# Some small steps of the softmax and of exp(q) from VectorE to ScalarE, with another order of work, in an attention plus gated MLP kernel

## The chip, the core and the metric

The kernel runs on one core of one Trainium2 chip. The metric is device time in microseconds (us) of one execution, as the median of several runs. The core's engines run side by side, each through its own queue in order: TensorE (PE in the profile; PEld is its weight load), VectorE (DVE), ScalarE (ACT), GpSimd (POOL) and SyncE (SP), which issues nearly all DMAs here. An engine that waits for another one stalls everything behind the waiting instruction in its own queue.

## The reference

Attention over 4 batches, 8 heads, 576 tokens and head size 64, with a causal softmax and a compressive memory, and then an MLP with a piecewise activation over the 2304 tokens (512 to 2048 to 512).

```python
scores = q @ k.T / 8, causal mask; scores -= scores.max(-1)
a = exp(scores); a /= a.sum(-1) + 1e-9; local = a @ v
q_p = where(q > 0, q, exp(q) - 1) + 1
mem_out = (q_p @ M_prev) / (q_p . z_prev + 1e-6)
x = g * mem_out + (1 - g) * local          # g = sigmoid(beta), per head
h = x @ w_in
g2 = where(h >= 1, h, where(h <= -1, 0, (h + 1)**2 / 4))
out = g2 @ w_out
```

## The kernel before

Every product is done in pairs of float16 halves: a float32 operand is scaled by a power of two, rounded to a high half, and the remainder is the low half; three matmuls (high by high, high by low, low by high) replace one. The scaling and the splitting are elementwise work for ScalarE (`mul`, line 107, with the engine "act": a Copy with a scale) and VectorE (`sub_scaled`, line 114).

The work is cut into jobs. There are 8 **pairs** (two units each) and 16 **units** (two heads of one batch each). `prep` (line 311) prepares a pair: squares for the scales, halves of k, q, v and the memory, and phi(q) with its normalisation, whose first steps stand at lines 347 to 352: Exp of q on ScalarE, the minimum with 1 on VectorE (line 350), then max(q + 1, that) on VectorE. Four times a unit, `front` (line 430) makes one tile of scores: matmuls and a mask on PE, a maximum over the row on VectorE (lines 444 and 462), `negmax` (line 421, its instruction is line 424) that multiplies the negated maxima, two, four or one number per partition, by the pair's scale, and `expsum` (line 426), the exponential on ScalarE with those maxima as its bias. `back` (line 487) makes the high and low halves of the probabilities by `halves` (line 480): the high half on ScalarE, except for row groups 6 and 7 (the 128x512 pieces of the fourth tile), whose high half is on VectorE by the table `OPT`, and then the low half on VectorE. A DMA transposes the halves, and `pv1` and `pv2` multiply them by the values. `half_a` of a unit does tokens 0 to 255, `half_b` the other 320.

The weights come in 8 groups (`weight_group`, line 178): three integer steps on VectorE for each of two matrices turn the input's 64-bit words into float32 (lines 201 to 203), ScalarE sums squares, and then come the halves. The MLP runs in 9 **chunks** of 256 tokens; `chunk_prep` makes a chunk's halves, and for each weight group `mlp_h` (line 634) does 24 matmuls into the tile h (line 646) and evicts it by a Relu and a Square on ScalarE (lines 651 and 652), a step on VectorE that also reads h (line 653), and the two halves of g; `mlp_o` (line 658) does 12 matmuls with g. The tile h has one buffer only: the next 24 matmuls wait until both readers of h are done.

The string `PROGRAM` (line 38) names the jobs in the order in which the program writes them: l load, P prep, A and B the halves of a unit, W a weight group, p chunk preparation, c a chunk (c0/4 is its first four weight groups alone). This isn't the order in which they run: `in_order` (line 906) takes all instructions, prices each with a table of costs, and lists them anew for every engine by 24 passes of a list schedule, forward and backward, and keeps the best of them. What the written order fixes is the first ranking, and the turns in which jobs take the buffers of a ring (`Rings`, line 83).

Of the kernel before, what the change touches and what calls it, by code (L numbers as in the profile page):

```python
# [20 lines left out]
AF = mybir.ActivationFunctionType  # L21
ALU = mybir.AluOpType
# [9 lines left out]

BLENDS = (-0.1,) * 24

OPT = dict(whi="act", phi="act", ghi="act", hi={6: "dve", 7: "dve"})


PROGRAM = ("l0 l1 P0 W0 A0 A1 P1 A2 A3 p0 W1 B0 W2 B1 W3 c0/4 B2 B3 p1 W4 l2 c1/4 W5 W6 W7 c0 c1 P2 A4 A5 l3 P3 "
           "A6 A7 l4 p2 B7 B4 B5 P4 c2 l5 B6 A9 p3 P5 c3 A8 l6 A10 A11 p4 B8 B9 P6 c4 B10 B11 l7 p5 P7 c5 A12 "
           "A14 A15 A13 B13 p6 B14 c6 B15 B12 p7 c7 p8 c8")  # L40

P = 128
D = 64
# [6 lines left out]
def infini_moe_kernel(ctx: ExitStack, tc, qt, kt, qz, vm, beta, w, out):  # L50
# [6 lines left out]
    nc = tc.nc  # L57
    NPP, _, _, S = qt.shape
# [44 lines left out]
    def kind(job, c):  # L103

        notes.append((len(nc.cur_bb.bb.instructions), job, c))

    def mul(n, o, i, s):
        if n == "act":
            return nc.scalar.activation(o, i, AF.Copy, scale=s)  # L109
        if n == "pool":  # L110
            return nc.gpsimd.tensor_scalar(o, i, s, 1.0, op0=ALU.mult, op1=ALU.mult)
        return nc.vector.tensor_scalar(o, i, s, None, op0=ALU.mult)

    def sub_scaled(o, i, s, hi):

        nc.vector.scalar_tensor_tensor(o, i, s, hi, op0=ALU.mult, op1=ALU.subtract)  # L116
# [61 lines left out]
    def weight_group(r):  # L178
# [36 lines left out]
        for m, wt in enumerate(words):  # L215
            reg, s = group(m, r), wsc[:, m, r:r + 1]
            hi, lo = reg[:, :, 0, :], reg[:, :, 1, :]
            wt = wt.rearrange("p (c f) -> p c f", f=reg.shape[3])
            mul(OPT["whi"], hi, wt, s)
            sub_scaled(lo, wt, s, hi)  # L220
# [90 lines left out]
    def prep(u):  # L311
        p, job = u.p, u.job
# [33 lines left out]

        kind(job, "ph")
        fe = sb.tile([P, 2, 9, D], F32, name=f"fe{p}", tag="pn")
        nc.scalar.activation(fe, u.qr, AF.Exp)
        nc.vector.tensor_scalar(fe, fe, 1.0, None, op0=ALU.min)  # L350
        ft = u.qr
        nc.vector.scalar_tensor_tensor(ft, u.qr, 1.0, fe, op0=ALU.add, op1=ALU.max)
        kind(job, "pz")
# [29 lines left out]
        fs = ft.rearrange("p u s d -> p (u s) d")  # L383
        mul(OPT["phi"], pn[:, :, 0, :], fs, 1.0)
        nc.vector.tensor_tensor(pn[:, :, 1, :], fs, pn[:, :, 0, :], op=ALU.subtract)
# [30 lines left out]
    def stats(u):  # L416
        if "st" not in u.e:
            u.e["st"] = sb.tile([P, 3, 9], F32, name=f"st{u.n}", tag="st")
        return u.e["st"]

    def negmax(u, a, m):

        st = stats(u)
        nc.vector.tensor_scalar(st[:, 0, a:a + m], st[:, 0, a:a + m], u.pair.cs, None, op0=ALU.mult)  # L424

    def expsum(u, e, s, z):
        st = stats(u)
# [52 lines left out]
    def halves(u, hi, lo, e, z):  # L480
        r = stats(u)[:, 2, z:z + 1]
        kind(u.job, "ah")
        mul(OPT["hi"].get(z, "act"), hi, e, r)
        kind(u.job, "al")
        sub_scaled(lo, e, r, hi)

    def back(u, i):
# [27 lines left out]
        else:  # L515
# [4 lines left out]
            kind(u.job, "ah")  # L520
            mul(OPT["hi"].get(8, "act"), flat[:, 0:S], e, r)
            kind(u.job, "al")
# [111 lines left out]
    def mlp_h(c, r, a, tb):  # L634
# [18 lines left out]
        nc.vector.scalar_tensor_tensor(tm, h, tb[:, 0, j:j + 1], tm, op0=ALU.max, op1=ALU.min)  # L653
        mul(OPT["ghi"], g16[:, 0], tm, tb[:, 3, j:j + 1])
        sub_scaled(g16[:, 1], tm, tb[:, 3, j:j + 1], g16[:, 0])
# [43 lines left out]
    preps, gens = {}, {}  # L699
    for n, t in enumerate(PROGRAM.split()):  # L700
        f, arg = t[0], t[1:]
# [20 lines left out]
        else:  # L722
            c, _, cuts = arg.partition("/")
# [100 lines left out]
def shape(ins):  # L824

    rd, wr = operands(ins)
    return 1 if rd[0].ap[0][1] == D else 2 if wr[0].ap[0][1] == D else 0


def graph(prog):  # L830

    before, banks = None, set()
    cost, needs, written, read = [], [], collections.defaultdict(list), collections.defaultdict(list)
    for k, ins in enumerate(prog):
        rd, wr = operands(ins)
        c, b = estimate(ins, rd, wr, before)
        if ins.engine.name == "PE":
            before = b
        cost.append(c)
        need = set()  # L840

        banks |= {a.tensor.name for a in rd + wr if a.space == bass.MemoryType.PSUM}
        spans = [(span(a), False) for a in rd if a.space != bass.MemoryType.DRAM] + \
                [(span(a), True) for a in wr if a.space != bass.MemoryType.DRAM]
        for (name, p0, p1, bits), w in spans:
            for j, a0, a1, m in written[name]:
                if a0 < p1 and p0 < a1 and m & bits:
                    need.add(j)
            if w or name in banks:
                for j, a0, a1, m in read[name]:  # L850
                    if a0 < p1 and p0 < a1 and m & bits:
                        need.add(j)
        for (name, p0, p1, bits), w in spans:
            if w:
                for acc in (written, read):
                    acc[name] = [x for x in acc[name] if x[1] < p0 or x[2] > p1 or x[3] & ~bits]
                written[name].append((k, p0, p1, bits))
        for (name, p0, p1, bits), w in spans:
            if not w:
                read[name].append((k, p0, p1, bits))  # L860
        need.discard(k)
        needs.append(need)
    return cost, needs
# [42 lines left out]
def in_order(tc, notes):  # L906

    prog, tags = [], []
    notes = iter(notes + [(math.inf, "", "")])
    tag, after = ("", ""), next(notes)
    for k, i in enumerate(tc.nc.cur_bb.bb.instructions):
        while k >= after[0]:
            tag, after = after[1:], next(notes)
        if (i.ins or i.outs) and type(i).__name__ not in ("InstRegisterMove", "BassTilePoolBoundary"):
            prog.append(i)  # L920
            tags.append(tag)
    n = len(prog)
    cost, needs = graph(prog)
    users = [[] for _ in prog]
    for k, need in enumerate(needs):
        for j in need:
            users[j].append(k)
    engine = [i.engine.name for i in prog]
    turns = ["Transpose" in type(i).__name__ for i in prog]
    mode = [shape(i) if e == "PE" else 0 for i, e in zip(prog, engine)]  # L930

    def forward(urgency):
        lane = busy = 0.0
        window, warm = 0, False

        def hold(e, k, at):
            nonlocal lane, busy, window, warm
            if e == "SP":
                at += 75 if needs[k] else 25
                lane = max(at + cost[k][0] + 650, lane) + cost[k][1]  # L940
                if turns[k]:
                    return lane, max(at + cost[k][0] + 525, lane - 952)
                return lane, max(at + cost[k][0], lane - AHEAD)
            took = cost[k]
            if e == "PE":
                while at >= (window + 1) * WINDOW:
                    warm = busy > 0.85 * WINDOW or warm and busy > 0.4 * WINDOW
                    busy = 0.0
                    window += 1
                if not warm:  # L950
                    took = 2 * took - 3 if took > 25 else 55
                busy += took
            return at + took, at + took

        return listed(n, engine, mode, [len(x) for x in needs], users, urgency, hold, lambda a, b: HOP[a][b], 650.0)

    def backward(urgency):
        def hold(e, k, at):
            if e == "SP":
                end = at + cost[k][1]  # L960
                return end + cost[k][0] + 725, max(end, at + 75 + cost[k][0] * 0.3)
            return at + cost[k], at + cost[k]

        return listed(n, engine, mode, [len(x) for x in users], needs, urgency, hold, lambda a, b: HOP[b][a], 0.0)

    urgency = [k - PRIO.get(c, 0) - PRIO.get(job, 0) - PRIO.get(job + c, 0) for k, (job, c) in enumerate(tags)]
    best, order = math.inf, None
    for blend in BLENDS:
        times, taken = forward(urgency)
        end = max(t[1] for t in times)  # L970
        if end < best:
            best, order = end, taken
        back, _ = backward([-t[1] for t in times])
        middle = sum(t[0] for t in times) / n
        urgency = [blend * (t[0] - middle) - b[1] for b, t in zip(back, times)]
    last = {}
    for k in order:
        e = engine[k]
        if e in last:
            tc.add_manual_dep(prog[k], last[e], mybir.DependencyInfo(mybir.DependencyClass.NoSync, mybir.DependencyReason.DATA), reason="order")  # L980
        last[e] = prog[k].name
# [46 lines left out]
```

## Time and profile before

| | us |
|---|---|
| median of 3 runs | 617.37 (616.97 to 619.64) |
| the profiled execution | 617.87 |
| its span, first to last instruction | 616.2 |

The profile's numbers are of the profiled execution, in us from the start of its span. A busy time is a recorded one; records of neighbours on DVE and ACT overlap a little, so what an instruction takes from its engine's time is the distance from its start to the start of the next one, where nothing waits. The granted clock is the share of full speed (2.4 GHz) that TensorE had; 0.5 is its lower level of 1.2 GHz.

### The profile page before, as it was taken

What the parts mean: (1) busy time and instruction counts of PE and PEld (TensorE: products, weight loads), DVE (VectorE), ACT (ScalarE), POOL (GpSimd) and SP (SyncE); (2) the same over time, 40 slices, a digit from 0 to 9 for tenths busy, and PEclk for the clock granted to TensorE, in tenths of its full rate; (3) what the DMA queues carried; (4) which work ended last, traced back from release to release, by engine and by line L of the source; (5) the groups of instructions that cost most, each with busy time, mean ns of one, the idle gap of its engine ahead of it and who ended that gap; (6) DMA issues with size and microseconds to landing.
All of it is one profiled execution on the core that took longest, in us unless ns stands there. A gap on an engine that the chain in (4) does not pass through costs nothing. (4 is left out here: it accounts for less than half of the span.)

```text
span 616.2 us, 11580 instructions
## 1 busy us (share of the span) xinstructions
PE 521.7 (85%) x4481; PEld 333.6 (54%) x4481; DVE 475.5 (77%) x1106; ACT 451.8 (73%) x916; POOL 2.5 (0%) x12
## 2 busy tenths in 40 slices
PE   0324565768699999999999999999999999999996
PEld 0112334444456566656665665666666666666663
DVE  5999999999999998497989849978677763223221
ACT  5768877769989987599797879769886765444433
POOL 1000000000000000000000000000000000000000
PEclk9997655799899999999999999999999999999999
DMA  7885984795542945348473526904362531000000
GB/s 307 294 273 135 231 207 126 201 216 212 145 103 62 183 95 97 91 124 199 134 160 63 112 59 154 220 3 83 69 106 50 126 67 32 35 1 2 35 0 35
DMA packets 130792, 74.68 MB, mean 121 GB/s; under 512 B 122289, under 2 KB 122289, under 8 KB 128689
## 3 DMA queue, kind: packets, MB, share of 16 engines
q1 hardware_dynamic: 130736, 73.94, 48.3%
q8 instruction: 35, 0.57, 0.4%
q14 instruction: 21, 0.16, 0.1%
HBM read 38.80 MB, written 4.72 MB: 71 GB/s over the span
## 5 line engine op out<-in xcount | busy, mean ns | idle before, releaser
L646 PE MATMUL h<-xh,w 128*128 128x256 f16 x1728 | 207.5, 276 | 12.8 <-DVE tm L653 12.1
L663 PE MATMUL o<-w,g 128*128 128x512 f16 x864 | 207.8, 379 | 6.7 <-DVE g L116 3.8
L646 PEld LDWEIGHTS <-w 128*128 128x128 f16 x1728 | 170.1, 99 | 51.3 <-issue 20.1
L663 PEld LDWEIGHTS <-g 128*128 128x128 f16 x864 | 80.7, 98 | 88.0 <-DVE g L116 5.3
L653 DVE SCALAR_TENSOR_TENSOR tm<-h,tb,tm 128x512 f32<-128x512 f32 x72 | 53.8, 747 | 68.7 <-ACT tm L652 64.2
L651 ACT ACTIVATE tm<-h,tb 128x512 f32<-128x512 f32 x72 | 55.8, 775 | 68.3 <-PE h L646 68.1
L428 ACT ACTIVATE e<-s,st,sc 128x256 f32<-128x256 f32 (+4 forms) x144 | 91.4, 638 | 13.4 <-DVE st L424 9.1
L116 DVE SCALAR_TENSOR_TENSOR an<-e,st,an 128x512 f16<-128x512 f32 (+4 forms) x160 | 80.8, 538 | 6.9 <-ACT an L109 6.9
L109 ACT ACTIVATE g<-tm,tb 128x512 f16<-128x512 f32 x72 | 51.8, 721 | 26.6 <-DVE tm L653 24.6
L116 DVE SCALAR_TENSOR_TENSOR g<-tm,tb,g 128x512 f16<-128x512 f32 x72 | 53.5, 746 | 18.9 <-ACT g L109 18.7
L109 ACT ACTIVATE an<-e,st 128x128 f16<-128x128 f32 (+3 forms) x112 | 56.0, 544 | 11.5 <-DVE st L478 3.8
L413 PE MATMUL s<-ks,qs 64*128 64x256 f16 (+3 forms) x384 | 43.4, 335 | 23.9 <-ACT e L428 8.8
L462 DVE TENSOR_REDUCE st<-s 128x2 f32<-128x256 f32 (+1 forms) x64 | 52.0, 816 | 5.5 <-PE s L458 5.3
L533 PEld LDWEIGHTS <-vs 128*64 128x64 f16 x1024 | 40.6, 118 | 17.0 <-issue 16.6
L652 ACT ACTIVATE tm<-tm 128x512 f32<-128x512 f32 x72 | 45.3, 629 | 1.0
L413 PEld LDWEIGHTS <-qs 64*128 64x128 f16 x384 | 16.1, 101 | 48.2 <-issue 27.3
L428 ACT ACTIVATION_READ_ACCUMULATOR e<-s,st,sc 128x1 f32 x144 | 28.9, 201 | 0.0
L533 PE MATMUL v<-eb,vs 128*64 128x256 f16 (+1 forms) x384 | 24.2, 276 | 2.1 <-DMA eb<-an 2.1
L533 PE MATMUL v<-pt,m 128*64 128x256 f16 (+1 forms) x192 | 19.2, 271 | 7.0 <-DMA pt<-pn 4.0
L307 PE MATMUL s<-sc,ones 128*128 128x4 f32 (+1 forms) x32 | 6.0, 263 | 21.9 <-ACT m L328 13.7
L109 ACT ACTIVATE w<-w,wsc 128x1024 f16<-128x1024 f32 x15 | 17.2, 1144 | 7.9 <-DVE nr L362 5.6
L204 ACT ACTIVATE stg<-w 128x1024 bf16<-128x1024 f32 x15 | 15.8, 1051 | 6.6 <-DVE w L203 6.4
(154 smaller groups left out, 575.7 us busy)
## 6 DMA issues: line engine op xcount, KB each, us to landing
stg<-w SPq DMA_DIRECT2D x16, 1024.0 KB, 5.5
rn<-qz SPq DMA_DIRECT2D x7, 768.0 KB, 5.3
rv<-vm SPq DMA_DIRECT2D x7, 768.0 KB, 5.0
rk<-kt SPq DMA_DIRECT2D x7, 576.0 KB, 4.1
rq<-qt SPq DMA_DIRECT2D x7, 576.0 KB, 5.0
out<-tm SPq DMA_DIRECT2D x14, 256.0 KB, 2.1
out<-part SPq DMA_DIRECT2D x4, 256.0 KB, 2.0
w<-vm SPq DMA_DIRECT2D x1, 768.0 KB, 13.8
```

The lines of the kernel that those rows point to most:

```text
L109: return nc.scalar.activation(o, i, AF.Copy, scale=s)
L116: nc.vector.scalar_tensor_tensor(o, i, s, hi, op0=ALU.mult, op1=ALU.subtract)
L204: nc.scalar.activation(stage.bitcast(BF16)[:, 0:w.shape[3]], wt, AF.Square, accum_out=ss[:, m:m + 1])
L413: nc.tensor.matmul(s[:, h, a:a + n], u.pair.q[hs, tq, u.x, i * P:(i + 1) * P], u.pair.k[hs, tk, u.x, 0:n], start=first and j == 0, stop=False)
L428: nc.scalar.activation(e, s, AF.Exp, bias=st[:, 0, z:z + 1], scale=u.pair.cs, accum_out=st[:, 1, z:z + 1])
L462: nc.vector.tensor_reduce(st[:, 0, 2 * t:2 * t + 2], s[:, :, a:a + P * (t + 1)], axis=AX.X, op=ALU.max, negate=True)
L533: nc.tensor.matmul(pv[h * D:(h + 1) * D, a:c1], lhs, rhs, start=n < 2, stop=n >= len(terms) - 2)
L646: nc.tensor.matmul(h[:, u], w1[:, r, cc, wj, u * P:(u + 1) * P], x16[:, xj, cc, :], start=n == 0, stop=n == 3 * NCC - 1)
L651: nc.scalar.activation(tm, h, AF.Relu, bias=tb[:, 1, j:j + 1], scale=tb[:, 2, j:j + 1])
L652: nc.scalar.activation(tm, tm, AF.Square)
L653: nc.vector.scalar_tensor_tensor(tm, h, tb[:, 0, j:j + 1], tm, op0=ALU.max, op1=ALU.min)
L663: nc.tensor.matmul(acc[:, t], g16[:, gj, u, t * P:(t + 1) * P], w2[:, r * FPG + u, wj, :], start=(r == a and u == 0 and gj == 0 and wj == ...
```

## The change

Four things change. `prep` makes min(exp(q), 1) in another way for all 8 pairs: a Relu of -q and an Exp of its negative, both on ScalarE, and no step on VectorE. `negmax` multiplies on ScalarE for all 16 units. The high halves of row groups 6 and 7 are on ScalarE for units 0 to 3, and stay on VectorE for units 4 to 15. And `PROGRAM` is another list of the same jobs. The planner's passes are put into a function that could be run again with noise; the list of seeds for this is empty, and the mean in it is taken by numpy.

```diff
-OPT = dict(whi="act", phi="act", ghi="act", hi={6: "dve", 7: "dve"})
+SEEDS = ()
+OPT = dict(whi="act", phi="act", ghi="act", hi={6: "dve", 7: "dve"}, neg=16, relu=8, hia=4)
-PROGRAM = ("l0 l1 P0 W0 A0 A1 P1 A2 A3 p0 W1 B0 W2 B1 W3 c0/4 B2 B3 p1 W4 l2 c1/4 W5 W6 W7 c0 c1 P2 A4 A5 l3 P3 "
-           "A6 A7 l4 p2 B7 B4 B5 P4 c2 l5 B6 A9 p3 P5 c3 A8 l6 A10 A11 p4 B8 B9 P6 c4 B10 B11 l7 p5 P7 c5 A12 "
-           "A14 A15 A13 B13 p6 B14 c6 B15 B12 p7 c7 p8 c8")
+PROGRAM = ("l0 l1 P0 A0 A1 P1 W0 A2 A3 p0 W1 B0 W2 B1 W3 c0/4 B2 B3 p1 W4 c1/4 W5 l2 W6 W7 c0 P2 A5 c1 l3 P3 A4 "
+           "A6 A7 p2 B7 B5 l4 B4 B6 P4 c2 l5 p3 A9 P5 c3 A8 B8 A10 A11 l6 p4 B9 P6 B10 B11 l7 c4 A12 p5 A13 P7 "
+           "c5 A14 A15 B13 p6 B14 c6 B15 B12 p7 p8 c8 c7")
...
-        nc.scalar.activation(fe, u.qr, AF.Exp)
-        nc.vector.tensor_scalar(fe, fe, 1.0, None, op0=ALU.min)
+        if p < OPT["relu"]:
+            nc.scalar.activation(fe, u.qr, AF.Relu, scale=-1.0)
+            nc.scalar.activation(fe, fe, AF.Exp, scale=-1.0)
+        else:
+            nc.scalar.activation(fe, u.qr, AF.Exp)
+            nc.vector.tensor_scalar(fe, fe, 1.0, None, op0=ALU.min)
...
-        nc.vector.tensor_scalar(st[:, 0, a:a + m], st[:, 0, a:a + m], u.pair.cs, None, op0=ALU.mult)
+        mul("act" if u.n < OPT["neg"] else "dve", st[:, 0, a:a + m], st[:, 0, a:a + m], u.pair.cs)
...
-        mul(OPT["hi"].get(z, "act"), hi, e, r)
+        mul(OPT["hi"].get(z, "act") if u.n >= OPT["hia"] else "act", hi, e, r)
```

## Rows read from the trace of the kernel before

**Rows 1.** The page's first part: busy time, share of the span and instructions of each engine.

```profile
PE 521.7 (85%) x4481; PEld 333.6 (54%) x4481; DVE 475.5 (77%) x1106; ACT 451.8 (73%) x916; POOL 2.5 (0%) x12
```

**Rows 2.** Busy time by stage: stretch, its length, busy time and instructions of PE, PEld, DVE, ACT and POOL, granted TensorE clock, share of the DMA engines' time, GB/s.

```profile
0.00:45.00 45.00, 9.51 (x71) 5.47 (x71) 37.44 (x87) 28.80 (x56) 2.49 (x12) 1.00 0.84 299
45.00:125.00 80.00, 47.16 (x413) 29.44 (x414) 78.59 (x177) 62.23 (x137) 0.00 (x0) 0.66 0.71 175
125.00:185.00 60.00, 47.73 (x381) 29.58 (x379) 59.96 (x139) 50.78 (x98) 0.00 (x0) 0.97 0.60 171
185.00:500.00 315.00, 307.81 (x2845) 198.38 (x2845) 260.12 (x630) 257.07 (x546) 0.00 (x0) 1.00 0.51 108
500.00:616.20 116.20, 109.52 (x777) 70.70 (x774) 39.40 (x77) 52.89 (x83) 0.00 (x0) 0.99 0.09 25
```

**Rows 3.** The same view, of four stretches of 5 us in which PE is idle longest between 125 and 160 us.

```profile
125.00:130.00 5.00, 2.28 (x22) 1.64 (x20) 5.00 (x12) 4.82 (x10) 0.00 (x0) 1.00 0.86 206
130.00:135.00 5.00, 2.92 (x23) 1.90 (x21) 5.00 (x9) 2.65 (x5) 0.00 (x0) 1.00 1.20 246
150.00:155.00 5.00, 3.59 (x24) 2.22 (x23) 5.00 (x11) 4.42 (x13) 0.00 (x0) 1.00 0.73 283
155.00:160.00 5.00, 1.68 (x16) 1.22 (x15) 5.00 (x11) 5.00 (x9) 0.00 (x0) 1.00 0.84 168
```

**Rows 4.** The instructions that VectorE loses, grouped by line and shape, in the stretches 0 to 131 us, 125 to 185 us and 185 to 500 us: count, busy us, mean ns of one, idle time before them. (The last of the 16 of line 424 in the first stretch begins at 123.94 us, so that none is in two stretches.)

```profile
L112 DVE TENSOR_SCALAR an<-e,st 128x512 f16<-128x512 f32 x8 | 3.6, 483 | 0.0
L350 DVE TENSOR_SCALAR pn<-pn 128x1152 f32<-128x1152 f32 x3 | 2.3, 752 | 5.2 <-ACT pn L349 5.2
L424 DVE TENSOR_SCALAR st<-st,sc 128x2 f32<-128x2 f32 x8 | 1.7, 221 | 0.0
L424 DVE TENSOR_SCALAR st<-st,sc 128x4 f32<-128x4 f32 x4 | 0.9, 217 | 0.0
L424 DVE TENSOR_SCALAR st<-st,sc 128x1 f32<-128x1 f32 x4 | 0.8, 208 | 0.0
...
L350 DVE TENSOR_SCALAR pn<-pn 128x1152 f32<-128x1152 f32 x1 | 0.8, 752 | 0.0
L424 DVE TENSOR_SCALAR st<-st,sc 128x4 f32<-128x4 f32 x2 | 0.4, 222 | 0.0
...
L424 DVE TENSOR_SCALAR st<-st,sc 128x2 f32<-128x2 f32 x24 | 5.2, 221 | 0.1
L350 DVE TENSOR_SCALAR pn<-pn 128x1152 f32<-128x1152 f32 x4 | 3.0, 759 | 1.9 <-ACT pn L349 1.9
L424 DVE TENSOR_SCALAR st<-st,sc 128x1 f32<-128x1 f32 x11 | 2.3, 208 | 0.0
L424 DVE TENSOR_SCALAR st<-st,sc 128x4 f32<-128x4 f32 x10 | 2.2, 220 | 0.0
```

**Rows 5.** The timeline of VectorE: start, us, line, operation, tiles and shapes. Each of lines 424, 350 and 112 with the instruction after it.

```profile
25.80 0.22 DVE L424 TENSOR_SCALAR st<-st,sc 128x4 f32<-128x4 f32 x1
25.93 0.68 DVE L201 TENSOR_SCALAR w<-stg 128x1024 int32<-128x1024 int32 x1
...
34.82 0.75 DVE L350 TENSOR_SCALAR pn<-pn 128x1152 f32<-128x1152 f32 x1
35.49 1.22 DVE L202 SCALAR_TENSOR_TENSOR w<-stg,w 128x1024 int32<-128x1024 int32 x1
...
84.69 0.48 DVE L112 TENSOR_SCALAR an<-e,st 128x512 f16<-128x512 f32 x1
85.08 0.17 DVE L212 CAST wh<-wi 128x2 f32<-128x2 int32 x1
```

**Rows 6.** The start of the first pair: the Exp on ScalarE, then the minimum and the step after it on VectorE.

```profile
5.25 1.16 ACT L349 ACTIVATE pn<-rn 128x1152 f32<-128x1152 f32 x1 [3.17 <-DMA rn<-qz]
...
6.44 0.76 DVE L350 TENSOR_SCALAR pn<-pn 128x1152 f32<-128x1152 f32 x1 [5.24 <-ACT pn L349]
7.24 1.36 DVE L352 SCALAR_TENSOR_TENSOR rn<-rn,pn 128x1152 f32<-128x1152 f32 x1
```

**Rows 7.** The timeline of ScalarE: a scaled copy of 128 columns with the next two; the Exp of line 349 with the next one; a half of 128x512 (line 109, g) with the next one; a Relu with the Square that needs its result; a Relu with an instruction after it that doesn't.

```profile
31.07 0.39 ACT L109 ACTIVATE an<-e,st 128x128 f16<-128x128 f32 x1
31.36 0.19 ACT L208 ACTIVATE wssb<-wss 128x2 bf16<-128x2 f32 x1
31.46 1.18 ACT L109 ACTIVATE an<-e,st 128x128 f16<-128x128 f32 x3
...
162.65 1.16 ACT L349 ACTIVATE pn<-rn 128x1152 f32<-128x1152 f32 x1
163.71 0.72 ACT L109 ACTIVATE g<-tm,tb 128x512 f16<-128x512 f32 x1
164.32 1.14 ACT L109 ACTIVATE w<-w,wsc 128x1024 f16<-128x1024 f32 x1
...
125.93 0.76 ACT L651 ACTIVATE tm<-h,tb 128x512 f32<-128x512 f32 x1
126.72 0.63 ACT L652 ACTIVATE tm<-tm 128x512 f32<-128x512 f32 x1
...
156.59 0.77 ACT L651 ACTIVATE tm<-h,tb 128x512 f32<-128x512 f32 x1
157.25 0.69 ACT L690 ACTIVATE part<-o,tu 128x512 f32<-128x512 f32 x1
```

**Rows 8.** Groups by line and shape over the span: two widths of the scaled copy on ScalarE, and the only load of an activation table.

```profile
L109 ACT ACTIVATE an<-e,st 128x256 f16<-128x256 f32 x32 | 15.0, 510 | 0.0
L109 ACT ACTIVATE an<-e,st 128x128 f16<-128x128 f32 x32 | 11.9, 403 | 3.5 <-issue 2.4 <-ACT e L428 0.8 <-DVE st L478 0.3
L349 ACT ACT_TABLE_LOAD x1 | 1.3, 1283 | 0.8 <-PEq L1019 0.8
```

**Rows 9.** Waits: who waited for whom, us in total, times, longest. The first is of VectorE between 45 and 125 us, the other two are of PE and ScalarE between 185 and 500 us.

```profile
DVE an L116 <- ACT an L109: 0.5, 1, 0.5
...
PE h L646 <- DVE tm L653: 3.8, 9, 0.9
...
ACT e L428 <- DVE st L424: 5.7, 5, 3.6
```

**Rows 10.** The timeline: the Exp of the third pair (P2) on ScalarE, and the last conversion of a weight group on VectorE.

```profile
64.73 1.15 ACT L349 ACTIVATE pn<-rn 128x1152 f32<-128x1152 f32 x1
...
158.40 1.22 DVE L203 SCALAR_TENSOR_TENSOR stg<-stg,stg 128x1024 int32<-128x1024 int32 x1
```

More of the change, by code (lines that the diff above doesn't have):

```diff
@@ L967, in in_order, with passes @@
     best, order = math.inf, None
[L968 to L975, printed above, removed]
+    def passes(urgency, blends):
+        nonlocal best, order, chosen
+        for blend in blends:
+            times, taken = forward(urgency)
+            end = max(t[1] for t in times)
+            if end < best:
+                best, order, chosen = end, taken, urgency
+            back, _ = backward([-t[1] for t in times])
+            middle = float(np.mean([t[0] for t in times]))
+            urgency = [blend * (t[0] - middle) - b[1] for b, t in zip(back, times)]
+    chosen = urgency
+    passes(urgency, BLENDS)
+    for seed, width in SEEDS:
+        noise = np.random.default_rng(seed).normal(size=n) * width
+        passes([u + float(x) for u, x in zip(chosen, noise)], BLENDS[:6])
     last = {}
```

## The prediction

> **What bounds the kernel now.** The first view is the page's line of engine totals: PE 85%, VectorE 77%, ScalarE 73% [rows 1]. No engine is full over the span, so the next view is busy time by stage, and the reader should look for the engine that is full in each [rows 2]. From 0 to 185 us VectorE has 175.99 of 185 us (37.44 + 78.59 + 59.96), nearly all of its idle time being the first load; PE has only 104.40 and so stands idle for 80.6 us. From 185 us on PE is full: idle for 7.2 of 315 us, then for 6.7 of 116.2 us, the end included. The time is therefore a start that VectorE sets, and then PE's fixed work with 14 us of gaps. What makes the start shorter moves the whole rest; what relieves VectorE after 185 us is worth nothing by itself. ScalarE is idle for 43.2 us of the first 185 (28.80 + 62.23 + 50.78 busy).
>
> A second loss lies in the start: the granted clock is 0.66 between 45 and 125 us, a mixture of the levels 1.2 and 2.4 GHz while PE works in short pieces, and 0.97 in the next stage [rows 2]. At full clock its 47.16 busy us would be some 16 us shorter; but PE waits there anyhow, so I count on none of that.
>
> **The change, part by part.** Every price is the distance to the next start.
>
> *Limit of exp(q).* Line 350 takes 0.67 us of VectorE (34.82 to 35.49) [rows 5]. It runs 4 times before 185 us and 4 times after [rows 4]. For the first pair VectorE is idle until the Exp is done; there the Relu delays the start: 5.25 + 1.05 for the Relu + 1.16 for the Exp + 0.04 gives 7.50 where line 352 now starts at 7.24, a loss of 0.26 [rows 6]. For the other three of the start: 3 x 0.67 = 2.01 gained. ScalarE gets a pass of 1152 columns each time, 1.06 us (162.65 to 163.71), and the Exp needs its result; such a pair costs a bubble: Relu to dependent Square is 0.79 us, to an independent instruction 0.66, so 0.13 more [rows 7]. That is 1.19 us for each pair. Relu, Exp, Square and Copy already alternate here with one table load in the whole span [rows 8], so I add none.
>
> *Scaling of the maxima.* 0.13 us of VectorE each (25.80 to 25.93) [rows 5]; 16 + 2 = 18 before 185 us, 45 in the next stage [rows 4]: 18 x 0.13 = 2.34 gained at the start. ScalarE has no such instruction now. Its scaled copy of 128 columns takes 0.29 us, of which 128 x (510 - 403) / 128 = 107 ns are columns [rows 7, 8]: about 0.18 is left. A plain copy of two columns takes 0.10 (31.36 to 31.46) [rows 7], the low bound; with the 0.13 bubble before the Exp that uses it, 0.31 is the high one, and I take it. The wait that comes with it: ScalarE now waits for the reduction itself instead of for line 424. What is queued behind is the same Exp, which waits for line 424 today (5.7 us in 5 times between 185 and 500 us) [rows 9]; the hop between engines is still one, so the chain of scores gets neither clearly longer nor shorter (-0.1 to +0.2 each).
>
> *High halves of groups 6 and 7, units 0 to 3.* 8 instructions, all before 131 us, of 0.39 us (84.69 to 85.08) [rows 4, 5]: 3.12 gained. ScalarE pays 0.61 each (163.71 to 164.32) [rows 7]. The low half, queued on VectorE, must now wait for ScalarE. Nothing shows this wait; its nearest row is the same pair of lines for the other groups, one wait of 0.5 us between 45 and 125 us [rows 9]. So 0 if something else is queued between, 8 x 0.5 = 4.0 if never; I take one wait, 0.5.
>
> *Order.* The written order is only the first ranking and the turn of buffers: P2 is written behind c0 and c1, but its Exp runs at 64.73, long before the weights are converted (158.40) [rows 10]. So W0 behind P1, l2 behind c1/4 and W5, and the swaps among A, B and c are no moves of the same size on the engines; l2's four loads, which pass W5's two on SP, can move by as little. I take 0. The bounds come from the gaps of the start: the two dips of PE from 125 to 135 and 150 to 160 us hold 4.8 + 4.7 = 9.5 us [rows 3]; a better order could close them, a worse one make as many.
>
> *Sum for VectorE before 185 us:* 2.01 - 0.26 + 2.34 + 3.12 - 0.5 = 6.7 us. ScalarE gets 4 x 1.19 + 18 x 0.31 + 8 x 0.61 = 15.2 us there, against 43.2 idle: it rises from 77% to some 88% of a start of 178 us, and VectorE stays the fuller one. What is late next is thus still VectorE. From 185 to 500 us ScalarE gets 45 x 0.31 + 4 x 1.19 = 18.7 us, 257.07 to 276 of 315 (82% to 88%); VectorE loses 45 x 0.13 + 4 x 0.67 = 8.5. The cover is PE's queue of other matmuls: today PE waits there for the release of h only 3.8 us in 9 times [rows 9]. I cost it at 0, with the rival below if that cover is gone.
>
> By 617.87 us of the profiled execution (1.67 more than its span) this gives 617.87 - 6.7 = 611.2 us. That execution lies 0.5 above the median of the runs, 617.37; I take 611.0.
>
> Rule against it: the Trainium skill, "ScalarE: Activation LUTs", section "Rules for kernel authors", says to keep relu, max, min and multiplications on VectorE, and to budget some 0.3 us for each ScalarE instruction before its columns. The trace agrees with the direction: 0.67 against 1.06, 0.13 against at most 0.31. By that rule as a whole, engine time is lost (34 us added to ScalarE for 17 taken from VectorE, as an estimate by my prices), which is the rival "slower".
>
> **The rivals.**
>
> *Nothing is left of it.* VectorE ends earlier, but a chain of ScalarE, DMA and VectorE sets the start: PE's dips are behind such chains, and from 155 to 160 us ScalarE is as full as VectorE, 5.00 of 5 us [rows 3]. The 15.2 us that come to ScalarE then give back the 6.7: 615 to 620, about 617.5. Against it: ScalarE has its idle time between 45 and 125 us, where most of the new work falls.
>
> *Slower.* Place: 185 to 500 us, the single buffer of h. ScalarE's queue is in order, and an instruction that waits for a reduction stands in front of the Relu that empties h. Price: 18.7 us if each addition delays the release of h, half of it, 9.3, as its middle: 611.2 + 9.3 = 620.5, up to 630. It decides from 6.7 / 18.7 = 36% of the added time on. For it: ScalarE would be the fullest engine beside PE. Against: of the 257 us of work that it does there, only 3.8 show up as a wait of PE for h [rows 2, 9].
>
> *More than the sum.* The start gets denser, the dips close and the lower clock lasts shorter: 611.2 - 9.5 = 601.7 with all dips closed. For it: the order was made with the new prices. Against: the program's planner doesn't see the chip.
>
> *Not as said.* The planner may list the instructions quite otherwise, so that lines 424 and 112 were never what stood in the way: this gives 617 again and is counted with the first rival.
>
> **How the numbers follow.** Forecast (606 to 614.3): 0.50. More than the sum (below 606): 0.15. Nothing left (614.3 to 620.5): 0.20. Slower (above 620.5): 0.15. 0.5%, about what a measurement of this kernel tells from no change, is 3.1 us: 614.3 and 620.5. Faster 0.65, same 0.20, slower 0.15. The range leaves out about a tenth at each end: from 602.5, nearly all dips closed, to 621, the first part of the slower rival.
>
> **What would show it.** By stage, the first stretch in which PE is idle for less than 5% should begin some 7 us earlier, with VectorE still full until then and ScalarE near 88%. No table load beyond the first. Lines 424 on ScalarE at 0.18 to 0.31 us from start to start. From 185 us on, PE's gaps should stay at 14 us, and its wait for h near 4 us. The forecast is wrong if VectorE shows new idle time behind ScalarE before 185 us (first rival), if PE waits for h or for scores over 10 us later on (slower), or if the first matmuls of c0 start at another place by far more than 7 us (the order, not the moved steps).

## The result, and the profile after

The changed kernel takes 602.98 us (median of 4 runs, 602.19 to 604.49) against 617.48 before: a ratio of 0.9762, with a 95% interval of 0.973 to 0.9793. That is 14.7 us less by the ratio (14.5 by the two medians) where I forecast 6.4; the time is just inside the range, the change is more than twice the forecast one. The profiled execution has 602.19 us and a span of 600.5.

The page's line of engine totals, to be read beside [rows 1]:

```profile
PE 518.0 (86%) x4481; PEld 333.3 (56%) x4481; DVE 457.4 (76%) x1026; ACT 476.4 (79%) x996; POOL 2.5 (0%) x12
```

VectorE lost 80 instructions and 18.1 us, ScalarE got 80 and 24.6 us. Busy time by stage, with the stretches of [rows 2] and the end at 600.5:

```profile
0.00:45.00 45.00, 9.97 (x77) 6.28 (x77) 36.60 (x89) 33.77 (x73) 2.49 (x12) 1.00 0.84 295
45.00:125.00 80.00, 47.70 (x418) 28.47 (x416) 79.32 (x162) 71.15 (x154) 0.00 (x0) 0.64 0.76 190
125.00:185.00 60.00, 55.39 (x458) 35.12 (x458) 60.00 (x144) 56.66 (x111) 0.00 (x0) 1.00 0.52 161
185.00:500.00 315.00, 309.66 (x2894) 201.97 (x2894) 251.37 (x576) 270.76 (x595) 0.00 (x0) 1.00 0.53 111
500.00:600.50 100.50, 95.23 (x644) 61.49 (x638) 30.10 (x58) 44.08 (x66) 0.00 (x0) 1.00 0.04 17
```

The reader should see four things. VectorE is as full up to 185 us as it was (175.92 us against 175.99): freed slots were filled with work that came later before. ScalarE has 161.6 of these 185 us, 87%, close to the 88% forecast. PE's idle time falls not only in the start (80.6 to 71.9 us, nearly all of it between 125 and 185 us) but also where I had left it alone: from 7.2 to 5.3 us between 185 and 500, and from 6.7 to 5.3 at the end. And PE's own busy time falls, from 521.7 to 518.0 us for the same 4481 matmuls. Between the two profiled spans (616.2 and 600.5 us) this makes 8.7 + 3.3 + 3.8 us: the start, the later gaps, the busy time. Where the 3.8 us come from was not taken apart.

The moved instructions themselves cost about what was forecast. On ScalarE's timeline, the first pair's Relu, its Exp and the next instruction; then a scaling of the maxima with its Exp, and one with work behind it that doesn't need its result:

```profile
5.21 1.16 ACT L352 ACTIVATE pn<-rn 128x1152 f32<-128x1152 f32 x1 [3.12 <-DMA rn<-qz]
6.40 1.16 ACT L353 ACTIVATE pn<-pn 128x1152 f32<-128x1152 f32 x1
7.47 1.15 ACT L330 ACTIVATE ks<-rk 128x1152 bf16<-128x1152 f32 x1
...
24.00 0.30 ACT L111 ACTIVATE st<-st,sc 128x4 f32<-128x4 f32 x1 [1.01 <-DVE st L468]
24.33 0.46 ACT L434 ACTIVATE e<-s,st,sc 128x128 f32<-128x128 f32 x1
...
48.74 0.28 ACT L111 ACTIVATE st<-st,sc 128x4 f32<-128x4 f32 x1
48.93 0.49 ACT L111 ACTIVATE an<-e,st 128x256 f16<-128x256 f32 x1
```

The Relu takes 1.19 us until its Exp can start (forecast 1.19), the first scaling 0.33 (forecast 0.31) and the second 0.19. Of all 64, from start to start, 44 take 0.19 to 0.20 us and 20 take 0.27 to 0.33, so the forecast 0.31 is nearly the dearest case. VectorE's first step after that Exp, which was at 7.24 [rows 6], starts at 7.60 (forecast 7.50):

```profile
7.60 1.36 DVE L358 SCALAR_TENSOR_TENSOR rn<-rn,pn 128x1152 f32<-128x1152 f32 x1 [6.39 <-ACT pn L353]
```

The groups of ScalarE by line and shape show that all 64 scalings are there, what they waited for, and that there is still one table load:

```profile
L111 ACT ACTIVATE st<-st,sc 128x2 f32<-128x2 f32 x32 | 9.4, 295 | 7.3 <-DVE st L468 6.8
L111 ACT ACTIVATE st<-st,sc 128x1 f32<-128x1 f32 x16 | 4.7, 294 | 0.0
L111 ACT ACTIVATE st<-st,sc 128x4 f32<-128x4 f32 x16 | 4.7, 291 | 5.9 <-DVE st L468 5.9
L352 ACT ACT_TABLE_LOAD x1 | 1.3, 1283 | 0.8 <-PEq L1035 0.8
```

Last, PE's waits between 185 and 500 us, of which [rows 9] has the first for the kernel before (3.8 us in 9 times):

```profile
PE h L652 <- DVE tm L659: 2.1, 6, 0.6
PE h L652 <- ACT xh L111: 1.3, 1, 1.3
PE v L539 <- DMA ec<-an: 0.8, 1, 0.8
```

The wait for the release of h, which I feared would grow, fell. Behind 500 us the kernel before had this wait too, and the changed one has none:

```profile
PE h L646 <- DVE tm L653: 1.4, 2, 0.8
```

So 3.1 of the 3.3 us by which PE's gaps behind 185 us shrank are this one wait (1.7 and 1.4).

### The profile page after: what moved, and what is told of

Same layout as the page of the kernel before. It is cut to its first block, busy times and chain, and to the rows that moved or that the text cites. A ratio compares the mean times of both kernels' runs of the same rounds, so it can differ in the third digit from the quotient of the medians.

```text
span 600.5 us, 11589 instructions
## 1 busy us (share of the span) xinstructions
PE 518.0 (86%) x4481; PEld 333.3 (56%) x4481; DVE 457.4 (76%) x1026; ACT 476.4 (79%) x996; POOL 2.5 (0%) x12
## 5 line engine op out<-in xcount | busy, mean ns | idle before, releaser
L652 PEld LDWEIGHTS <-w 128*128 128x128 f16 x1728 | 169.3, 99 | 45.6 <-issue 14.7
L111 ACT ACTIVATE an<-e,st 128x128 f16<-128x128 f32 (+4 forms) x120 | 62.4, 556 | 3.6 <-DMA eb<-an 1.6
L419 PE MATMUL s<-ks,qs 64*128 64x384 f16 (+3 forms) x384 | 42.5, 332 | 23.1 <-ACT e L434 7.8
L468 DVE TENSOR_REDUCE st<-s 128x2 f32<-128x768 f32 (+2 forms) x64 | 51.2, 813 | 0.9 <-PE s L464 0.8
L111 ACT ACTIVATE st<-st,sc 128x2 f32<-128x2 f32 (+2 forms) x64 | 18.8, 294 | 13.2 <-DVE st L468 12.7
L309 PE MATMUL s<-sc,ones 128*128 128x4 f32 (+1 forms) x32 | 5.7, 257 | 19.9 <-ACT m L330 13.7
L118 DVE SCALAR_TENSOR_TENSOR w<-w,wsc,w 128x1024 f16<-128x1024 f32 x15 | 19.1, 1275 | 0.0
## 6 DMA issues: line engine op xcount, KB each, us to landing
w<-vm SPq DMA_DIRECT2D x1, 768.0 KB, 12.1
```

Of the source, the lines that this page charges most:

```text
L309: nc.tensor.matmul(pt[:, 0:m], ones32, sc[:, a:a + m], start=True, stop=True)
L419: nc.tensor.matmul(s[:, h, a:a + n], u.pair.q[hs, tq, u.x, i * P:(i + 1) * P], u.pair.k[hs, tk, u.x, 0:n], start=first and j == 0, stop=False)
L468: nc.vector.tensor_reduce(st[:, 0, 2 * t:2 * t + 2], s[:, :, a:a + P * (t + 1)], axis=AX.X, op=ALU.max, negate=True)
L652: nc.tensor.matmul(h[:, u], w1[:, r, cc, wj, u * P:(u + 1) * P], x16[:, xj, cc, :], start=n == 0, stop=n == 3 * NCC - 1)
```

## The experiments

Three theories stood at the start. **Slots**: the moves are worth VectorE's freed time before 185 us, 6.7 us, and something else (the order) brought the rest. **Order**: the written order brings most. **More than slots**: the moves bring all, in a way that my sum missed. Differences below are ratios to the kernel before on the same chip, times 618 us.

### Which part: order alone, moves alone, and the luck of a plan

The planner makes new lists for each of these. In the changed kernel, order alone:

```diff
-OPT = dict(..., neg=16, relu=8, hia=4)
+OPT = dict(..., neg=0, relu=0, hia=0)
```

> The changed kernel with the three moves undone: limit of exp(q), scaling of the maxima and all high halves of groups 6 and 7 back on VectorE; only the written order of jobs is new, and the planner makes its lists for it. The result was 14.5 us faster than before, my sum gave 6.7. Theory 1 (the moves are worth their 6.7 us and the written order brings the rest): 609.5 to 611. Theory 2 (the order is worth nothing, the moves together bring all of it): 616 to 619. If the order brings nearly all: 603 to 606.

Measured: 618.48 us, ratio 1.0005 (0.999 to 1.0021). The written order alone is worth nothing.

The moves with the old `PROGRAM`:

> The three moves with the written order of the kernel before; the planner makes its lists for the moved work. Theory 1 (moves 6.7 us, order the rest): 610 to 612. Theory 2 (the moves bring all): 602 to 605. If the moves are hidden behind chains of ScalarE and DMA: 615 to 618.

Measured: 607.39 us, 0.9836 (0.981 to 0.9862), 10.1 us gained: between the two theories.

How far two plans of the same work lie apart, with another blend in the kernel before, in the changed one, and in the moves with the old order:

```diff
-BLENDS = (-0.1,) * 24
+BLENDS = (-0.12,) * 24
```

> The kernel before with the same work and the same written order, and only the planner's blend at -0.12 in place of -0.1, which gives another list of the same instructions. It measures how far two plans of the same work lie apart. If plans are alike: within 3 us of 617.5. If the luck of a plan is as large as the 8 us that my sum lacks: more than 5 us away on either side.

> The changed kernel with the planner's blend at -0.12 in place of -0.1: same work, same written order, another list. The moves alone with the old written order gave 607.4, the changed kernel 603. If those 4 to 5 us are the written order's, this stays at 602 to 605; if they are the chance of one plan, it lies anywhere from 602 to 609, and about 607 is as likely as 603.

> The three moves with the old written order and the blend at -0.12. If the written order makes 4 to 5 us: 606 to 609 again. If chance of plans: 602 to 609, and the two blends with the new order and the two with the old one overlap.

Measured: 617.46 (0.9988, 0.9973 to 1.0004), 604.22 (0.9776, 0.9752 to 0.98) and 608.75 (0.9847, 0.983 to 0.9865). Each plan lies within 0.0014, 0.9 us, of its sibling, the plan of the same work with the other blend. So the 4.5 us between old and new written order with the moves (0.9836 and 0.9847 against 0.9762 and 0.9776) show up under both blends; a difference of that size between siblings wasn't seen. In these plans, two of each kind with the moves and one of the new order without them, the written order is worth 4.5 us with the moves and nothing without them.

### The same moves in the old queues

The planner can be told another engine and price for an instruction than it has. Here it plans the moved work as if it were on VectorE, so that PE's and SP's queues are those of the kernel before, instruction for instruction, and a moved instruction stands in ScalarE's queue at the place where VectorE's list had it:

```diff
+def as_if(nc, e, price):
+    AS[nc.cur_bb.bb.instructions[-1].name] = (e, price)
...
-    engine = [i.engine.name for i in prog]
+    engine = [AS.get(i.name, (i.engine.name,))[0] for i in prog]
...
+        if u.n < OPT["neg"]:
+            as_if(nc, "DVE", 126 + 0.52 * m)
```

(and likewise for the second Exp and the high halves).

> The three moves, but the planner is told that the moved instructions still run on VectorE at VectorE's price: so the queues of PE, SP and of all other work are in the order of the kernel before, instruction for instruction, and each moved instruction stands in ScalarE's queue where VectorE would have had it. This prices the moves without any new plan. By my sum: 617.5 - 6.7 = about 611, with VectorE's stage before 185 us ending some 6 to 7 us earlier. If the gain needs a plan made for it: 614 to 618. If the moves are worth the whole result: 603.

Measured: 625.58 us, 1.0121 (1.0098 to 1.0143), 7.5 us slower than before. All theories failed here. Its busy time by stage, to be read against [rows 2]:

```profile
45.00:125.00 80.00, 45.01 (x415) 28.00 (x416) 74.51 (x153) 70.01 (x159) 0.00 (x0) 0.79 0.72 177
125.00:185.00 60.00, 48.81 (x361) 29.60 (x361) 56.92 (x128) 51.37 (x100) 0.00 (x0) 0.91 0.58 169
185.00:500.00 315.00, 302.86 (x2772) 194.09 (x2769) 252.83 (x583) 268.28 (x586) 0.00 (x0) 1.00 0.50 107
```

VectorE, idle there for 1.4 and 0.0 us before, is now idle for 5.5 and 3.1 us in the first two of these stretches. Its queue still has the old order, so it stands before instructions that wait for ScalarE, low halves and the reciprocals of the sums, instead of doing other work in the freed time. Its two longest waits between 45 and 125 us:

```profile
DVE an L125 <- ACT an L118: 2.9, 5, 0.9
DVE st L492 <- ACT e L444: 2.4, 4, 1.0
```

The first was 0.5 us in one time before [rows 9]. PE, however, loses most of its time later. Its idle time up to 185 us is 81.7 us against 80.6, and between 185 and 500 us 12.1 against 7.2. Two of its waits in that stretch:

```profile
PE h L664 <- DVE tm L671: 4.9, 9, 1.1
PE s L453 <- ACT e L444: 2.3, 3, 1.4
```

The first was 3.8 us before. How the later loss comes about was not taken apart. This kernel and the moves planned anew do the same work with the same written order, and lie 17.6 us apart by their lists alone.

### Each move by itself, planned anew

With the new written order (whose own value is nothing), only the maxima, only the limit, only the maxima of units 0 to 3, only those of units 4 to 15:

> New written order, only the scaling of the maxima on ScalarE (64 instructions), planned anew. By slots of VectorE before 185 us alone: 18 x 0.13 = 2.3 us off 618.5, so 616. If a scaling that stands in the full queue of VectorE between the reduction and the exponential costs more than its slot: 610 to 613.

> New written order, only the limit of exp(q) on ScalarE (8 pairs), planned anew. By slots before 185 us: 3 x 0.67 - 0.26 = 1.75 us off 618.5, so 616.7. If every move that frees VectorE brings a plan several us better, whatever the size of the move: 611 to 614.

> Only the scaling of the maxima on ScalarE and only for units 0 to 3: 16 instructions, all before 131 us. By slots 16 x 0.13 = 2.1 us: 616. If the first 16 carry the value of the whole move, since VectorE sets the start: 607 to 610. If the value lies in the 48 later ones: 614 to 618.

> Only the scaling of the maxima on ScalarE and only for units 4 to 15: 48 instructions, nearly all behind 185 us, where PE is full. By my document this is worth nothing: 617 to 619. If the later ones shorten PE's gaps as well: 612 to 615.

Measured: 607.41 (0.9834, 0.9808 to 0.9859), 611.29 (0.9893, 0.9872 to 0.9914), 607.93 (0.9839, 0.9822 to 0.9856) and 613.34 (0.9925, 0.9901 to 0.995): 10.3, 6.6, 9.9 and 4.6 us gained. Each is far more than its slots before 185 us, and they don't add up: the first 16 maxima and the other 48 give 9.9 + 4.6 by themselves and 10.3 together. The last one shows that moves in the stage that I wrote off are worth something.

Is it the slot on VectorE, or one crossing less (a place where the chain from reduction to exponential enters the queue of another engine)? The maxima on ScalarE, and 64 slots of the same width given back to VectorE where no crossing is added:

```diff
+        mul("dve", st[:, 2, a:a + m], st[:, 2, a:a + m], ones32[:, 0:1])
         nc.vector.reciprocal(st[:, 2, a:a + m], st[:, 2, a:a + m])
```

> As the kernel that moved only the scaling of the maxima (607.4), with its 64 slots given back to VectorE elsewhere: a multiplication by one of the same width on the reciprocal's input, between two steps that are on VectorE anyway, so that it takes VectorE's time but adds no crossing in the chain from reduction to exponential. If the freed slots are what counts: 615 to 618.5. If the place in the chain counts (one pass less through VectorE's full queue): 607 to 610.

Measured: 613.65 us, 0.9937 (0.9914 to 0.9959). Of the 10.3 us, 6.4 go with the slots, 3.9 stay. It falls between the theories, and since this kernel has a plan of its own, the 3.9 us can't be put down to the chain.

### The moves undone in the new queues

This takes the planner out. The moved instructions go back to VectorE, but are planned as if on ScalarE; PE's and SP's queues are then those of the changed kernel, instruction for instruction, and so is the order of all other work on VectorE and ScalarE. All three undone, then only the early ones, only the late ones, only one kind each:

```diff
-        mul("act" if u.n < OPT["neg"] else "dve", st[:, 0, a:a + m], ...)
+        mul("dve", st[:, 0, a:a + m], ...)
+        as_if(nc, "Activation", 186 + 0.834 * m)
```

> All three moves undone, but the planner is told that the instructions still run on ScalarE at its price: PE, SP and all other queues are in the order of the changed kernel. If that order by itself is better and the moves only led the planner to it: 603 to 607. If the order is good only with the moved work off VectorE: the 7 us of slots or more come back, 610 to 620.

> The changed kernel's lists, every queue in its order, and only the early moves undone: maxima of units 0 to 3, limits of pairs 0 to 3 and the eight high halves are back on VectorE, planned as if on ScalarE. All three undone in this way gave 616.4, 13.4 us more than 603. If VectorE's slots before 185 us are worth what I summed, 6.7 to 8 us: 609.5 to 611. If they carry all of it: 615 to 617.

> The same lists with only the late moves undone: maxima of units 4 to 15 and limits of pairs 4 to 7 back on VectorE. My document costed these at nothing: 603. If VectorE's work behind 185 us lengthens PE's gaps: 606 to 608.

> The same lists with only the scaling of the maxima, all 64, back on VectorE. By slots 18 x 0.13 = 2.3 us before 185 us: 605.5. If a crossing of VectorE's full queue in the chain from reduction to exponential costs more than a slot, or the later 45 cost too: 608 to 612.

> The changed kernel's lists with only the scaling of the maxima of units 4 to 15 back on VectorE, the limits stay on ScalarE. All late moves undone gave 609.9. If the maxima are what counts there: 609 to 610. If the four limits have a part by their slots (4 x 0.67 of 8.5 us): 607 to 608.

> The same lists with only the eight high halves of groups 6 and 7 of units 0 to 3 back on VectorE. By slots 8 x 0.39 - 0.5 = 2.6 us: 605.5. If ScalarE's longer half (0.61 us) was in the way as much: 603.

> The changed kernel's lists with only the limit of exp(q) of all 8 pairs back on VectorE. By slots before 185 us 3 x 0.67 - 0.26 = 1.75 us, with the four later ones at the same rate some 4: 605 to 607. If the undone moves add up (all 13.4, maxima 9.4, high halves 4.4), nothing is left for it: 602.5 to 603.5, since ScalarE's longer work in the chain of a pair takes back what VectorE gains.

Measured, with the cost against the changed kernel's 0.9762:

| undone | median us | ratio (95%) | cost us |
|---|---|---|---|
| all three | 616.40 | 0.9979 (0.9965 to 0.9992) | 13.4 |
| early moves | 609.53 | 0.9867 (0.9847 to 0.9886) | 6.5 |
| late moves | 609.86 | 0.9876 (0.9855 to 0.9897) | 7.0 |
| all maxima | 612.38 | 0.991 (0.9892 to 0.9928) | 9.1 |
| maxima of units 4 to 15 | 608.90 | 0.9854 (0.9837 to 0.9871) | 5.7 |
| high halves | 607.34 | 0.9825 (0.9809 to 0.9841) | 3.9 |
| limit of exp(q) | 604.69 | 0.9774 (0.9757 to 0.979) | 0.7 |

Each cost carries the uncertainty of both ratios, some 2 to 3 us. Within it they add up in fixed queues: early and late give 13.5, the three kinds 13.7, against 13.4 for all. The limit of exp(q) can't be told from nothing (the interval holds 0.9762); the early and the late part are both clear of zero.

A cost of this kind could also come from a bad place: an undone instruction stands in VectorE's queue where ScalarE's list had it. For the maxima, the late moves' larger part, the trace of the late moves undone shows no wait before them:

```profile
L121 DVE TENSOR_SCALAR st<-st,sc 128x2 f32<-128x2 f32 x24 | 5.2, 221 | 0.0
L121 DVE TENSOR_SCALAR st<-st,sc 128x4 f32<-128x4 f32 x12 | 2.7, 222 | 0.0
L121 DVE TENSOR_SCALAR st<-st,sc 128x1 f32<-128x1 f32 x12 | 2.5, 206 | 0.0
```

Where the late part lies is in the same trace. Its stage of 185 to 500 us, and the longest wait of PE there:

```profile
185.00:500.00 315.00, 304.64 (x2816) 198.04 (x2814) 258.84 (x625) 256.11 (x543) 0.00 (x0) 1.00 0.52 108
...
PE h L664 <- DVE tm L671: 6.6, 12, 1.1
```

PE is idle for 10.4 us instead of 5.3, and 4.5 of these 5.0 us are one wait: for VectorE's step that releases h, 6.6 us in 12 times against 2.1 in 6. With the early moves undone, the loss lies in the start instead:

```profile
0.00:45.00 45.00, 8.65 (x69) 5.58 (x71) 37.37 (x93) 30.38 (x67) 2.49 (x12) 1.00 0.82 283
45.00:125.00 80.00, 42.40 (x402) 25.56 (x398) 79.66 (x176) 61.27 (x129) 0.00 (x0) 0.67 0.72 187
125.00:185.00 60.00, 54.70 (x432) 34.43 (x430) 59.22 (x135) 50.74 (x100) 0.00 (x0) 0.93 0.57 167
185.00:500.00 315.00, 309.89 (x2859) 201.58 (x2858) 256.11 (x591) 275.36 (x605) 0.00 (x0) 1.00 0.52 109
```

PE is idle for 79.3 us up to 185 us, 7.3 more than with all the moves, and no longer than with them between 185 and 500 us (5.1 against 5.3).

## Why the prediction was wrong

**What bounds the start, and its sum: right.** VectorE stayed the full engine, ScalarE rose to 87%, and undoing the early moves in fixed queues costs 6.5 us where the sum said 6.7 (6.5 without the two early maxima of later units, which that run leaves on ScalarE). That the sum fits so well is partly luck, since its terms don't: the high halves cost 3.9 us for 2.6 (3.12 less the wait of 0.5), the maxima of units 0 to 3 cost 9.1 - 5.7 = 3.4 for 2.1 (16 x 0.13), and the limit 0.7 in all for 1.75 in the start alone. With 2 to 3 us of uncertainty on each, no single term is shown wrong.

**"What relieves VectorE after 185 us is worth nothing by itself": the step that failed.** It rested on PE being full there and on its wait for h being only 3.8 us [rows 2, 9]. Late moves are worth 7.0 us in the new queues, most of the 8.9 us (48 x 0.13 + 4 x 0.67) that they take from VectorE. PE does have other matmuls, but its queue is in order too: when VectorE comes late to the step that frees h, PE stands. I took the short wait of 3.8 us as a sign that PE's other matmuls cover VectorE there; in the changed kernel's queues the same wait is 6.6 us with the late moves undone and 2.1 us with them. So the 7.0 us are what the late moves are worth in the new lists. Against the kernel before, whose lists are others, PE's gaps behind 185 us shrank by 3.3 us. The wait was of VectorE's step, as [rows 9] says in its line, while my rival put ScalarE's in its place and looked only for what it could add.

**The order: value 0, bounds 9.5.** Alone it is worth 0 (618.48 us), and the new lists with the work unmoved are worth 1.3 us (0.9979). With the moves, the new order gives 4.5 us over the old one under both blends. So order and moves aren't two terms of a sum; I had no term for what they give together. New lists, early and late moves give 1.3 + 6.5 + 7.0 = 14.8 us, beside the 14.7 measured; with 2 to 3 us of uncertainty on a term, so close a fit is luck.

**"More than the sum": the time that came, by half of its mechanism.** The measured time lies below 606 us, as this rival had it. The start did get denser: PE's idle time between 125 and 185 us, where the dips were, fell from 12.3 to 4.6 us. The last long stretch at the lower clock also ended sooner, at 98 instead of 106 us:

```profile
68.80:106.40 37.60, 22.35 (x195) 13.01 (x195) 36.20 (x84) 28.16 (x59) 0.00 (x0) 0.50 0.69 177
...
50.80:98.30 47.50, 26.04 (x217) 14.05 (x216) 46.82 (x94) 43.66 (x95) 0.00 (x0) 0.50 0.81 208
```

(The first line is of the kernel before, the second of the changed one.) But the start as a whole gave only 8.7 us. What went beyond that lies in PE's later gaps and in its busy time, of which the rival says nothing.

**"Not as said" and "nothing is left of it".** I let the freed slots become a shift of the whole rest without asking whose list lets VectorE do so. In the old queues the same moves cost 7.5 us. The first rival's mechanism (VectorE waits for ScalarE) shows there in 5.5 and 3.1 us of idle time, though 4.9 of the 6.6 us between the profiled spans (622.8 and 616.2) are idle time of PE between 185 and 500 us. With lists made for the moves, the freed time was filled with other work.

**"Slower".** Its wait fell from 3.8 to 2.1 us although ScalarE rose from 82% to 86% of that stage (270.76 of 315). The rule against the change (the Trainium skill, "ScalarE: Activation LUTs", "Rules for kernel authors") was right on the direction of the prices, 0.19 to 0.33 against 0.13 us for a scaling. Its budget of about 0.3 us is for an ACTIVATE whose bias is a pointer; the scalings here, with a pointer as scale, are recorded at 0.29 to 0.30 us. The time went the other way: with lists made for them, 80 dearer instructions on the engine with idle time were cheaper than 80 cheap ones on the engine that PE waits for.

**What stays open.** Planned anew, the first 16 maxima alone gain 9.9 us, with slots of 2.1 us; in fixed queues the early maxima cost 3.4. What differs is the planner's list for that work, but which of its places make the difference wasn't taken apart. Nor is it settled whether 3.9 of the 10.3 us of the maxima belong to one crossing less of VectorE's queue, why the written order counts only together with the moves, or where the 3.8 us of PE's busy time went: the kernel before with the other blend has 519.6 us of it, 2.1 less than the kernel before, in the same time.

## What to carry to other kernels

An engine that is busy for 80% of a stage isn't free there when the full engine's in-order queue waits on it: price its slots at the wait that ends on it, in both directions, before writing "worth nothing". When instructions move between engines with fixed queues, the move and the lists are one change: ask for each freed slot what stands next in that queue and whether it is ready. And to price such a move alone, undo it while every other queue keeps its order; planned anew, parts here gave 9.9 + 4.6 us for a whole of 10.3.

## What the runs showed of the hardware

The mean granted clock of an execution is no guide to its time here. The changed kernel's four runs had 0.951, 0.988, 0.952 and 0.974 of full speed and took 602.19, 604.49, 602.38 and 603.58 us. Of 52 executions of the kernel before (0.95 to 0.992), the 32 with a mean below 0.975 have a median of 618.1 us and the 20 others one of 618.2.

One reason shows in the trace with only the high halves undone, whose mean is 0.989. It shows 1.00 for the whole of 45 to 96 us, a stretch that in the profiled run of the changed kernel is at 0.50 from 50.8 us on. But the matmuls of one form (line 445 of the changed kernel, 455 of this one, 128x512) are as long in the one as in the other, 613 ns. Where the changed kernel's granted clock is 1.00, between 185 and 500 us, they take 380 ns:

```profile
45.00:96.00 51.00, 28.67 (x241) 15.39 (x241) 50.77 (x104) 42.85 (x96) 0.00 (x0) 1.00 0.80 205
L455 PE MATMUL s<-ks,diag 128*128 128x512 f16 x9 | 4.7, 613 | 0.0
...
L445 PE MATMUL s<-ks,diag 128*128 128x512 f16 x9 | 4.7, 613 | 0.0
...
L445 PE MATMUL s<-ks,diag 128*128 128x512 f16 x36 | 11.0, 380 | 0.0
```

(The first two lines are of the trace with the high halves undone, from 45 to 96 us; the others are of the changed kernel, from 50.8 to 98.3 and from 185 to 500 us.) So a 1.00 in the start of a profile can stand over matmuls that run at the length of the lower level. The first stretch in the tables above is such a case too: in the changed kernel the 128x128 matmuls of line 464 take 308 ns up to 47 us, where the profile shows 1.00, and 222 ns between 185 and 500 us. The share of 0.66 in the prediction is therefore to be read with care: the 16 us that the prediction worked out from 0.66 are not shown, and what the lower clock costs in the start was not measured.
